# Attention, mixing and a Strassen feed-forward on one core: the mixing split in two, eight pairs of q left unscaled, and a new order table

## The chip, the cores and the metric

The kernel runs on one core of one Trainium2 chip. The metric is the device time of one execution in microseconds (us). The engines are named as the profile names them: PE is TensorE (PEld its weight loads), DVE is VectorE, ACT is ScalarE, POOL is GpSimd, SP is SyncE.

## The reference

Attention with a soft cap over 4 batches of 12 heads, 448 positions, 64 channels a head, then a block in which the positions are mixed through rank 32 and each position goes through a feed-forward layer of 768 to 3072 to 768 channels. All in float32.

```python
scale = 1.0 / np.sqrt(q.shape[-1])
scores = scale * np.matmul(q, k.transpose(0, 1, 3, 2))
scores = cap * np.tanh(scores / cap)
attn = np.exp(scores - np.max(scores, axis=-1, keepdims=True))
attn = attn / (np.sum(attn, axis=-1, keepdims=True) + 1e-09)
x = np.matmul(attn, v)                         # then heads side by side: [4, 448, 768]
...
xt = x.transpose(0, 2, 1)
h = xt @ U @ V                                 # U [448, 32], V [32, 448]
u = x + h.transpose(0, 2, 1)
out = u + np.maximum(u @ w_ch1, 0.0) @ w_ch2
```

## The kernel before, in words

Heads are taken in pairs, 24 pairs p in all, two heads in the 128 partitions of one tile: `qk` is [2 heads x 64, q or k, 448]. Each call of `four(p)` makes the work of four pairs. For each pair, score products of 128 keys at a time (L548) go into two PSUM banks, `tanh` reads them (L555, on ACT), one `exp` covers two such tiles (L566), and A·V products (L597) follow. The last 64 keys of two pairs share a tile (the rests: scores in tiles of 64x64, their A·V at L621). The finished sums of a pair are copied into `u[b]`, still unnormalized (a helper does every copy: L312 on ACT, L314 on DVE). The factor 1/(cap * sqrt(64)) of the scores is the column `qsc`: q of all pairs but the first is multiplied by it on DVE (L524); for the first pair, tanh takes it as its `scale`, from memory (`raw`).

`normalize(p)` works on two pairs. The row sums of exp are added up over tiles on DVE (L603, into `es`) and over partitions on PE (the sums, L646, tiles of 128x32, into the PSUM tile `misc`); they are copied to `sr`, spread by a transfer, inverted (L662), written to memory and read back broadcast as `rb`; then `u` is multiplied by `rb` (L675). Three transfers lie in that chain, on the queue of POOL.

`mixin(b, pp)` mixes one such two pairs, twelve times in all: 16 transposes (L696, tiles of 64x112), copies of them into `xx`, 8 U products (L712, tiles of 112x32), a copy into `ys`, 2 V products (L723, 64x128), and two adds onto `u` on DVE (L730). `misc` has two banks, and sums (one bank), transposes (two), U products (one) and V products (two) take turns in them.

After that, `moe` computes the feed-forward with Strassen's seven products in place of eight, both layers (L865 up, L1011 down), in products of 128x128 by 448 columns; operands are sums of blocks of `u` and of the weights, made on DVE, ACT and POOL, and stored and loaded through memory.

No order is written out by hand as a whole. Every piece of work is a `task` with a guessed duration, what it reads and writes, and a priority. `simulate()` plays the tasks through with the guessed durations and gives each a place in one program order. `NUDGE` changes some priorities, `SIDES` sets the engine of copies that ACT and DVE can both do, and `MOVES`, pairs (i, j), takes task i out of the order and puts it ahead of task j. The engines then run their instructions in that order and wait for one another by semaphores. A task's `mode` is the tile shape that the planner counts it under, and a name such as `("sums", p)` in a read list makes a task come behind the one that writes it.

Of the kernel before, what the change touches and what calls it, by code (L numbers as in the profile page):

```python
# [38 lines left out]
ALONE = 12  # L39


NUDGE = {89: 3, 194: 8, 248: -8, 361: -1, 440: 8, 653: 8, 717: -5, 782: -5, 823: 1}
MOVES = (
# [19 lines left out]
)  # L63
SIDES = {
    79: "DVE", 196: "DVE", 257: "DVE", 281: "ACT", 286: "ACT", 490: "ACT", 549: "ACT", 585: "ACT", 587: "ACT",
    625: "DVE", 666: "DVE", 670: "DVE", 774: "DVE",
}
NEXT = 8
LATER = 0
RESTS = 24  # L70
FILL, FIRST = 11, 3


# [245 lines left out]
class Build(Plan):  # L319
# [155 lines left out]
    def attention(self):  # L475

        u = self.u_bufs = [
            self.buf("u%d" % b, [128, NP, S], F32, self.ua if b < 2 else self.up) for b in range(B)]  # L480
        thirds = [lambda t, i=i: t[:, i:i + 2] for i in (0, 2, 4)]
        self.gw = Pool("gw", {"gq": 3}, after=(self.wx,), within=(self.wx, "x"), parts=(F32, [128, NP, S], {"gq": thirds}))
        self.es, self.rest = {}, {}
        for p in range(0, B * NP, 4):
            self.four(p)
            for q in (p, p + 2):
                self.normalize(q + 1)
                if q > 2:
                    self.mixin((q - 4) // NP, (q - 4) % NP // 2)
        for q in (B * NP - 4, B * NP - 2):  # L490
            self.mixin(q // NP, q % NP // 2)

    def psum(self, tag, n=1):
        pool = self.px if tag in ("sc2", "o2") else self.ps
# [2 lines left out]
    def four(self, p):  # L497
# [6 lines left out]
        for i in range(4):  # L504
            b, q = divmod(p + i, NP)
            if i % 2 == 0:
                vn = self.buf("vn", [128, 7, 2, D], F32, self.ap)
                vns.append(vn)
            qk = self.buf("qk", [128, 2, S], F32, *pools)
            qks.append(qk)  # L510

            if p + i == 0:
                cut = S + 128
                for a, z in ((0, cut), (cut, 2 * S)):
                    self.task({"SP": 350}, lambda a=a, z=z, b=b, q=q, qk=qk: nc.sync.dma_start(
                        out=qk.t.rearrange("p a s -> p (a s)")[:, a:z], in_=self.qk[b, q].rearrange("p a s -> p (a s)")[:, a:z]),
                        w=[(qk, 0 if a == 0 else "k")], lat=3400, prio=-2000 if a == 0 else prios[i])
                    if a == 0:
                        self.scales()
            else:  # L520
                self.task({"SP": 350}, lambda b=b, q=q, qk=qk: nc.sync.dma_start(out=qk.t, in_=self.qk[b, q]), w=[(qk, 0)],
                    lat=3400 if p == 0 else 4200, prio=prios[i])
            if p or i:
                self.task({"DVE": 360}, lambda qk=qk: nc.vector.tensor_scalar(  # L524
                    out=qk.t[:, 0], in0=qk.t[:, 0], scalar1=self.qsc, scalar2=None, op0=ALU.mult), r=[("scale", 0)], w=[(qk, 0)],
                    prio=prios[i])
            if i % 2:
                self.task({"SP": 350}, lambda b=b, q=q, vn=vn: nc.sync.dma_start(out=vn.t, in_=self.v[b, q // 2]),
                    w=[(vn, 0)], lat=4000, prio=prios[i], begin=6000 if p == 0 else 0)
# [3 lines left out]
        for g in range(7):  # L533
# [3 lines left out]
            for j in range(2):  # L537
# [11 lines left out]
                                ps.t[out, a, :S], qks[c].t[hd, 1, 128 * t:min(S, 128 * t + 128)], qks[c].t[hd, 0],  # L549
                                start=True, stop=True)  # L550

                raw = p == 0 and i == 0 or cs == (0, 1) and p == 0

                def tanh(j=j, ps=ps, th=th, raw=raw, t=t):
                    nc.scalar.activation(  # L555
                        out=th.t[:, j], in_=ps.t[:, :, :S], func=AF.Tanh, scale=(self.half if t == 3 else self.qsc) if raw else 1.0)

                r = [(qks[c], 0) for c in cs] + ([(qks[0], "k")] if p == 0 and t and 0 in cs else [])
                if j == 0:
# [120 lines left out]
    def mixin(self, b, pp):  # L680
# [15 lines left out]
                        nc.tensor.transpose(  # L696
                            tps[a].t[:TM, at:at + 64], u.t[hd, 2 * pp + i, TM * t:TM * t + TM], self.ident[hd, hd])

        self.task({"PE": 480}, transposes, r=[*ks, ("ident", 0)], w=[(tp, 0) for tp in tps], prio=prio, mode="sc")
        for a, tp in enumerate(tps):  # L700
            self.task({"ACT": 520, "DVE": 640}, lambda e, a=a, tp=tp: self.copy(
                e, xx.t.rearrange("p t i n -> p (t i) n")[:, :, 64 * a:64 * a + 64],
                tp.t[:TM].rearrange("p (m n) -> p m n", n=64)), r=[(tp, 0)], w=[(xx, a)], prio=prio)
        yp = self.psum("misc")

        def products():
# [5 lines left out]
                        nc.tensor.matmul(  # L712
                            yp.t[rows, :128], self.ust.t[:, t, :R], xx.t[:, t, i], start=h == 0, stop=h == 1)

        self.task({"PE": 450}, products, r=[(xx, 0), (xx, 1), (self.ust, 0), ("sums", p + 4)], w=[(yp, 0)], prio=prio - (20 if p < 19 else 0), mode="s")
        ys = self.buf("ys", [128, 128], F32, self.an)
        self.task({"ACT": 240, "DVE": 250}, lambda e: self.copy(e, ys.t, yp.t[:, :128]), r=[(yp, 0)], w=[(ys, 0)], prio=prio)
        hs = [self.psum("misc") for _ in range(2)]
# [375 lines left out]
```

## Time and profile before

| | us |
|---|---|
| median of 3 runs | 809.11 |
| lowest and highest | 808.36, 809.12 |
| the profiled execution | 810.04 |
| its span (first to last instruction) | 808.3 |
| busy in the span: PE, DVE, ACT, POOL | 798.9, 679.7, 472.0, 111.9 |

The busy times are for the whole span and hide that the attention part (to about 208 us) has other limits than the feed-forward behind it: ACT is busy 58% of the span, but nearly all of its first 60 us. A busy PE is one with work in its pipeline; PEld, the weight loads, overlaps it.

### The profile page before, as it was taken

What the parts mean: (1) busy time and instruction counts of PE and PEld (TensorE: products, weight loads), DVE (VectorE), ACT (ScalarE), POOL (GpSimd) and SP (SyncE); (2) the same over time, 40 slices, a digit from 0 to 9 for tenths busy, and PEclk for the clock granted to TensorE, in tenths of its full rate; (3) what the DMA queues carried; (4) which work ended last, traced back from release to release, by engine and by line L of the source; (5) the groups of instructions that cost most, each with busy time, mean ns of one, the idle gap of its engine ahead of it and who ended that gap; (6) DMA issues with size and microseconds to landing.
All of it is one profiled execution on the core that took longest, in us unless ns stands there. A gap on an engine that the chain in (4) does not pass through costs nothing.

```text
span 808.3 us, 11887 instructions
## 1 busy us (share of the span) xinstructions
PE 798.9 (99%) x4344; PEld 638.5 (79%) x4344; DVE 679.7 (84%) x1084; ACT 472.0 (58%) x669; POOL 111.9 (14%) x182
## 2 busy tenths in 40 slices
PE   9999999999999999999999999999999999999998
PEld 4333333437899999999999999999999999999997
DVE  3869999999999879998778683899999988897663
ACT  7999999976656455655555563435444543433330
POOL 0111111111111111111111121011100011000100
PEclk9999999999999999999999999999999999999999
DMA  7365575315877888547777864966973688524142
GB/s 236 118 215 157 168 232 138 117 47 151 290 270 258 296 298 286 198 139 237 276 259 236 280 209 135 388 219 166 367 244 104 163 260 256 150 61 115 38 134 92
DMA packets 54525, 161.76 MB, mean 200 GB/s; under 512 B 7458, under 2 KB 21314, under 8 KB 54466
## 3 DMA queue, kind: packets, MB, share of 16 engines
q1 hardware_dynamic: 34736, 106.82, 40.6%
q0 software_dynamic: 12816, 35.30, 15.3%
q10 hardware_dynamic: 6914, 18.88, 5.9%
q8 instruction: 34, 0.56, 0.3%
q14 instruction: 25, 0.20, 0.1%
HBM read 106.81 MB, written 46.49 MB: 190 GB/s over the span
## 4 chain that ended last, share of the span: by engine, by line
PE 83%; DVE 8%; ACT 4%; DMA 3%; issue 2%; POOL 0%; ACTq 0%; DVEq 0%; POOLq 0%
PE mm L1011 38%; PE mm L865 36%; PE sc L548 4%; DVE es L603 3%; PE o L597 3%; ACT th L555 2%; DMA r<-sr 2%; DMA qk<-in_qk 1%; ACT th L566 1%; DVE u L730 1%; DMA mid<-cx 1%; PE misc L468 1%; DVE ws L763 1%; PE misc L723 1%; DVE u L675 1%
## 5 line engine op out<-in xcount | busy, mean ns | idle before, releaser
L865 PE MATMUL mm<-x,ws 128*128 128x448 f32 x1404 | 288.8, 365 | 0.4 <-ACT cx L312 0.3
L865 PEld LDWEIGHTS mm<-x,ws 128*128 128x128 f32 x1404 | 262.7, 188 | 24.8 <-ACT cx L312 1.9
L1011 PE MATMUL mm<-g,wl 128*128 128x448 f32 x570 | 148.9, 364 | 0.0
L1011 PEld LDWEIGHTS mm<-g,wl 128*128 128x128 f32 x570 | 107.0, 188 | 8.7
L1031 DVE TENSOR_TENSOR u<-u,mm 128x448 f32<-128x448 f32 x111 | 67.5, 616 | 41.0 <-PE mm L1011 38.4
L1011 PE MATMUL mm<-g,bw 128*128 128x448 f32 x420 | 101.4, 366 | 0.0
L891 POOL DMA_DIRECT2D mid<-cx x96 | 54.0, 562 | 256.8 <-ACT cx L312 246.8
L1011 PEld LDWEIGHTS mm<-g,bw 128*128 128x128 f32 x420 | 78.9, 188 | 6.3
L1011 PE MATMUL mm<-gk,bw 128*128 128x448 f32 x336 | 83.0, 367 | 0.0
L548 PE MATMUL sc<-qk 64*128 64x448 f32 (+1 forms) x384 | 77.6, 569 | 0.3 <-ACT th L555 0.3
L312 ACT ACTIVATE cx<-mm 128x448 f32<-128x448 f32 x96 | 48.8, 543 | 47.6 <-PE mm L865 32.3
L566 ACT ACTIVATE th<-th,capt 128x1792 f32<-128x1792 f32 x42 | 75.5, 1798 | 0.9
L555 ACT ACTIVATE th<-sc 128x896 f32<-128x896 f32 x80 | 69.8, 919 | 4.9 <-PE sc L548 4.6
L1011 PEld LDWEIGHTS mm<-gk,bw 128*128 128x128 f32 x336 | 63.1, 188 | 5.5
L312 ACT ACTIVATE cx<-cx 128x448 f32<-128x448 f32 x72 | 41.6, 577 | 43.6 <-DVE cx L878 40.5
L1036 POOL DMA_DIRECT2D u<-st x33 | 28.5, 875 | 247.0 <-ACT st L312 229.3
L878 DVE TENSOR_TENSOR cx<-cx,mm 128x448 f32<-128x448 f32 x72 | 44.4, 617 | 20.9 <-PE mm L865 18.1
L548 PEld LDWEIGHTS sc<-qk 64*128 64x128 f32 (+1 forms) x384 | 27.7, 175 | 41.5 <-issue 21.0
L597 PE MATMUL o<-th,vn 128*64 128x448 f32 x280 | 57.9, 548 | 0.9 <-ACT th L566 0.9
L312 ACT ACTIVATE st<-mm 128x448 f32<-128x448 f32 x33 | 17.9, 544 | 68.9 <-PE mm L1011 31.0
L603 DVE TENSOR_TENSOR es<-es,th 128x896 f32<-128x896 f32 (+1 forms) x48 | 51.8, 1079 | 4.7 <-ACT th L566 4.0
L1011 PE MATMUL mm<-gk,wl 128*128 128x448 f32 x186 | 55.8, 365 | 0.0
(110 smaller groups left out, 1039.1 us busy)
## 6 DMA issues: line engine op xcount, KB each, us to landing
wr<-in_w SPq DMA_DIRECT2D x48, 768.0 KB, 6.1
mid<-cx POOLq DMA_DIRECT2D x96, 224.0 KB, 4.0
gq<-mid SPq DMA_DIRECT2D x44, 448.0 KB, 7.0
qk<-in_qk SPq DMA_DIRECT2D x23, 448.0 KB, 4.1
kept<-wa ACTq DMA_DIRECT2D x24, 384.0 KB, 6.3
quad<-wa ACTq DMA_DIRECT2D x24, 384.0 KB, 6.2
wb<-quad SPq DMA_DIRECT2D x24, 384.0 KB, 8.4
wa<-kept SPq DMA_DIRECT2D x24, 384.0 KB, 4.4
```

The source lines that it names most:

```text
L312: e.activation(out=out, in_=in_, func=func)
L548: nc.tensor.matmul(ps.t[out, a, :S], qks[c].t[hd, 1, 128 * t:min(S, 128 * t + 128)], qks[c].t[hd, 0], start=True, stop=True)
L555: nc.scalar.activation(out=th.t[:, j], in_=ps.t[:, :, :S], func=AF.Tanh, scale=(self.half if t == 3 else self.qsc) if raw else 1.0)
L566: nc.scalar.activation(out=th.t, in_=th.t, func=AF.Exp, scale=self.capt)
L597: nc.tensor.matmul(o.t[64 * a:64 * a + 64, :S], vn.t[:, 3 * i + t, a], th.t[:, j, a], start=t == 0, stop=False)
L603: e.tensor_tensor(out=out(), in0=in0(), in1=in1(), op=ALU.add)
L865: nc.tensor.matmul(ps.t[:, :S], ws[p].t[:, wi, sl], xs[p].t[:, xi, d], start=fresh and n == 0, stop=n == 8, skip_group_check=not fresh)
L878: self.task({"DVE": 630}, lambda: nc.vector.tensor_tensor(out=to(x), in0=to(x), in1=bank[onto].t[:, :S], op=ALU.add), r=[key(x), (bank[ont ...
L891: nc.gpsimd.dma_start(out=self.mid[at][:, c % 2], in_=to(x))
L1011: nc.tensor.matmul(ps.t[:, :S], w[p, m].t[:, wi, k, sl], g[p, n, m][gi].t[:, k], start=fresh and i == 0, stop=i == len(at) - 1, skip_group ...
L1031: self.task({"DVE": 622}, lambda: nc.vector.tensor_tensor(out=out(), in0=out(), in1=ps.t[:, :S], op=ALU.add), r=[(ps, 0)], w=[key], prio=-200)
L1036: self.task({"POOL": 1000}, lambda: nc.gpsimd.dma_start(out=out(), in_=st.t, accum_op=ALU.add), r=[(st, 0)], w=[key], lat=5000, size=1360, ...
```

## The change

First, `mixin` stops once, between the copies of the transposes and the U products, and `attention` runs the first half of one mix ahead of the sums of a later two pairs and its second half behind them: the mix is now that of six pairs back (it was four). The U products wait for the sums of that later pair by name, where they waited for an earlier one, and have no priority of their own any more. Three mixes are left for the end of attention, where there were two. Second, q of the pairs from `PLAIN` = 16 on is not multiplied on DVE; their 28 tanh take `qsc` as `scale`. Third, `NUDGE` is empty and `MOVES` and `SIDES` hold other numbers.

```diff
-NUDGE = {89: 3, 194: 8, 248: -8, 361: -1, 440: 8, 653: 8, 717: -5, 782: -5, 823: 1}
+NUDGE = {}
 MOVES = (
-    (1993, 1994), (1974, 1993), (1997, 2001), (1992, 1997), (1928, 1989), (1985, 1972), (1969, 1983), (1970, 1969),
...
+    (2046, 2070), (2003, 2025), (2023, 2024), (2018, 1999), (2021, 2018), (2002, 2021), (1964, 2015), (1929, 1964),
...
+PLAIN = 16
...
             for q in (p, p + 2):
+                mixed = self.mixin((q - 6) // NP, (q - 6) % NP // 2) if q >= 6 else iter(())
+                next(mixed, None)
                 self.normalize(q + 1)
-                if q > 2:
-                    self.mixin((q - 4) // NP, (q - 4) % NP // 2)
-        for q in (B * NP - 4, B * NP - 2):
-            self.mixin(q // NP, q % NP // 2)
+                next(mixed, None)
+        for q in (B * NP - 6, B * NP - 4, B * NP - 2):
+            for _ in self.mixin(q // NP, q % NP // 2):
+                pass
...
-            if p or i:
+            if (p or i) and p < PLAIN:
                 self.task({"DVE": 360}, lambda qk=qk: nc.vector.tensor_scalar(
...
-                raw = p == 0 and i == 0 or cs == (0, 1) and p == 0
+                raw = p == 0 and i == 0 or cs == (0, 1) and p == 0 or p >= PLAIN
...
-                        out=th.t[:, j], in_=ps.t[:, :, :S], func=AF.Tanh, scale=(self.half if t == 3 else self.qsc) if raw else 1.0)
+                        out=th.t[:, j], in_=ps.t[:, :, :S], func=AF.Tanh, scale=(self.half if t == 3 and p == 0 else self.qsc) if raw else 1.0)
...
+        yield
         yp = self.psum("misc")
...
-        self.task({"PE": 450}, products, r=[(xx, 0), (xx, 1), (self.ust, 0), ("sums", p + 4)], w=[(yp, 0)], prio=prio - (20 if p < 19 else 0), mode="s")
+        self.task({"PE": 450}, products, r=[(xx, 0), (xx, 1), (self.ust, 0), *([("sums", p + 6)] if p + 6 < B * NP else [])], w=[(yp, 0)], prio=prio - 0, mode="s")
```

In the rows below `misc`, `sc` and `o` are PSUM tiles (a number marks which one of several), and a row such as "128x448 x2" is two instructions of 128 by 448. Lines after L524 stand three to five further down in the changed kernel: L548 is L551, L597 is L600, L646 is L649, L696 is L699, L712 is L716 and L723 is L727.

On PE, in the middle of attention, around one round of sums, transposes, U and V products. Before:

```order
L646 MATMUL misc<-es,ones 32x448 x4
L548 MATMUL sc<-qk 128x448 x2
L548 MATMUL sc_1296<-qk 128x448 x2
L696 MATMUL misc<-ident,u_1016 112x64 x16
L597 MATMUL o<-th,vn 64x448 x6
L712 MATMUL misc<-xx,ust 32x128 x8
L548 MATMUL sc<-qk 128x448 x2
L548 MATMUL sc_1358<-qk 128x448 x2
L723 MATMUL misc<-vst,ys 128x448 x2
L597 MATMUL o_1381<-th,vn 64x448 x6
```

And of the change:

```order
L649 MATMUL misc<-es,ones 32x448 x4
L716 MATMUL misc<-xx,ust 32x128 x8
L551 MATMUL sc<-qk 128x448 x2
L551 MATMUL sc_1286<-qk 128x448 x2
L727 MATMUL misc<-vst,ys 128x448 x2
L600 MATMUL o<-th,vn 64x448 x6
L699 MATMUL misc<-ident,u_996 112x64 x16
L551 MATMUL sc<-qk 128x448 x2
L551 MATMUL sc_1346<-qk 128x448 x2
L600 MATMUL o_1360<-th,vn 64x448 x6
```

The U products have moved up to the sums. The transposes of the next mix stand where V products of this one are one A·V task back.

On PE, at the end of attention, where the first products of the feed-forward (L865, now L869) come in. Before:

```order
L696 MATMUL misc<-ident,u_1016 112x64 x16
L597 MATMUL o<-th,vn 64x448 x6
L597 MATMUL o_1623<-th,vn 64x448 x6
L712 MATMUL misc<-xx,ust 32x128 x8
L621 MATMUL o<-th,vn 64x448 x2
L621 MATMUL o_1623<-th,vn 64x448 x2
L723 MATMUL misc<-vst,ys 128x448 x2
L865 MATMUL mm<-x,ws 128x448 x9
L646 MATMUL misc<-es,ones 32x448 x4
L865 MATMUL mm<-x,ws 128x448 x9
```

And of the change:

```order
L727 MATMUL misc<-vst,ys 128x448 x2
L600 MATMUL o<-th,vn 64x448 x6
L699 MATMUL misc<-ident,u_996 112x64 x16
L600 MATMUL o_1609<-th,vn 64x448 x6
L624 MATMUL o<-th,vn 64x448 x2
L624 MATMUL o_1609<-th,vn 64x448 x2
L869 MATMUL mm<-x,ws 128x448 x9
L649 MATMUL misc<-es,ones 32x448 x4
L716 MATMUL misc<-xx,ust 32x128 x8
L869 MATMUL mm<-x,ws 128x448 x9
L727 MATMUL misc<-vst,ys 128x448 x2
```

V products and transposes stand ahead of the last A·V task, where the U products stood behind it.

On ACT, between three of the last dozen exps (L566, now L569; tanh is L555, now L558; copies are L312, now L313). Before:

```order
L566 ACTIVATE th<-th,capt 128x1792
L555 ACTIVATE th<-sc 128x896
L555 ACTIVATE th<-sc_1266 128x896
L312 ACTIVATE u_1016<-o 128x448
L312 ACTIVATE u_1016<-o_1248 128x448
L312 ACTIVATE sr<-misc 128x448
L566 ACTIVATE th<-th,capt 128x1792
L312 ACTIVATE xx<-misc 112x8x64
L555 ACTIVATE th<-sc 128x896
L555 ACTIVATE th<-sc_1296 128x896
L312 ACTIVATE bx<-xc 128x448
```

And of the change:

```order
L569 ACTIVATE th<-th,capt 128x1792
L558 ACTIVATE th<-sc,qsc 128x896
L558 ACTIVATE th<-sc_1240,qsc 128x896
L313 ACTIVATE u_996<-o_1226 128x448
L313 ACTIVATE sr<-misc 128x448
L313 ACTIVATE ys<-misc 128x128
L569 ACTIVATE th<-th,capt 128x1792
L558 ACTIVATE th<-sc,qsc 128x896
L558 ACTIVATE th<-sc_1286,qsc 128x896
L313 ACTIVATE x<-u_271 128x448
```

Every tanh there takes `qsc`; one copy into `u`, the copy of transposes and the one into `bx` are gone from this piece, and one of U products and one of `x` have come.

## Rows read from the trace of the kernel before

**Rows 1.** The first line of the profile's page.

```profile
span 808.3 us, 11887 instructions
```

**Rows 2.** Stretches: length, busy us of PE, PEld, DVE, ACT, POOL; granted clock; DMA.

```profile
8.08:61.45 53.37, 52.71 (x319) 19.17 (x318) 36.83 (x54) 52.62 (x50) 6.56 (x11) 1.00 0.56 177
61.45:131.50 70.05, 69.06 (x526) 26.55 (x524) 67.11 (x102) 64.77 (x69) 11.60 (x20) 1.00 0.57 175
131.50:175.06 43.56, 42.54 (x308) 16.38 (x304) 43.33 (x70) 43.29 (x49) 6.76 (x12) 1.00 0.37 106
175.06:208.37 33.31, 31.52 (x242) 21.40 (x242) 32.41 (x58) 20.90 (x44) 5.99 (x11) 1.00 0.57 167
208.37:804.60 596.23, 596.20 (x2934) 550.62 (x2934) 497.95 (x792) 286.95 (x457) 80.32 (x125) 1.00 0.66 214
```

**Rows 3.** Waits of PE, 17 to 209 us: total, times, longest.

```profile
PE o L597 <- ACT th L566: 0.9, 1, 0.9
PE misc L723 <- ACT ys L312: 0.9, 2, 0.5
PE misc L723 <- DVE ys L314: 0.8, 3, 0.4
PE misc L646 <- DVE u L730: 0.5, 1, 0.5
PE misc L696 <- DVE u L675: 0.4, 1, 0.4
PE sc L548 <- ACT th L555: 0.3, 1, 0.3
PE misc L712 <- DVE xx L314: 0.2, 1, 0.2
```

**Rows 4.** Timeline of PE, 149 to 172 us: start, us, engine and line.

```profile
149.97 1.77 PE L548 MATMUL sc<-qk 64*128 64x448 f32 x8
151.68 0.98 PE L621 MATMUL o<-th,vn 64*64 64x448 f32 x8
...
155.97 2.48 PE L597 MATMUL o<-th,vn 128*64 128x448 f32 x12
158.38 0.64 PE L712 MATMUL misc<-xx,ust 112*32 112x128 f32 x16
158.95 1.77 PE L548 MATMUL sc<-qk 64*128 64x448 f32 x8
160.56 0.92 PE L723 MATMUL misc<-vst,ys 64*128 64x448 f32 x4
161.31 1.67 PE L548 MATMUL sc<-qk 64*128 64x448 f32 x8
...
168.82 1.77 PE L548 MATMUL sc<-qk 64*128 64x448 f32 x8
170.43 0.62 PE L696 MATMUL misc<-ident,u 64*112 64x64 f32 x16
170.98 1.35 PE L597 MATMUL o<-th,vn 128*64 128x448 f32 x6
```

**Rows 5.** Groups by line and form, whole span: busy us, mean ns.

```profile
L555 ACT ACTIVATE th<-sc 128x896 f32<-128x896 f32 x80 | 69.8, 919 | 4.9 <-PE sc L548 4.6
...
L524 DVE TENSOR_SCALAR qk<-qk,qsc 128x448 f32<-128x448 f32 x23 | 10.0, 440 | 8.3 <-DMA qk<-in_qk 8.2
...
L555 ACT ACTIVATE th<-sc,qsc 128x896 f32<-128x896 f32 x3 | 3.0, 1002 | 3.2 <-PE sc L548 3.2
```

**Rows 6.** The same view for ACT, 131.5 to 175.06 us.

```profile
L312 ACT ACTIVATE u<-o 128x448 f32<-128x448 f32 x5 | 2.7, 570 | 0.0
...
L312 ACT ACTIVATE bx<-xc 128x448 fp32r<-128x448 f32 x1 | 0.6, 637 | 0.0
```

**Rows 7.** Timeline, 102 to 108 us.

```profile
103.05 1.67 PE L548 MATMUL sc<-qk 64*128 64x448 f32 x8
...
106.36 1.15 DVE L730 TENSOR_TENSOR u<-u,misc 128x448 f32<-128x448 f32 x2
```

More of the change, by code (lines that the diff above doesn't have):

```diff
@@ L39 @@
 ALONE = 12
-NUDGE = {89: 3, 194: 8, 248: -8, 361: -1, 440: 8, 653: 8, 717: -5, 782: -5, 823: 1}
+NUDGE = {}
 MOVES = (
[19 rows of a table removed]
[19 rows of a table added]
 )
 SIDES = {
-    79: "DVE", 196: "DVE", 257: "DVE", 281: "ACT", 286: "ACT", 490: "ACT", 549: "ACT", 585: "ACT", 587: "ACT",
-    625: "DVE", 666: "DVE", 670: "DVE", 774: "DVE",
+    79: "DVE", 80: "ACT", 171: "DVE", 263: "ACT", 279: "ACT", 360: "DVE", 370: "ACT", 562: "ACT", 577: "ACT",
+    579: "ACT", 587: "ACT", 593: "ACT", 595: "ACT", 625: "ACT", 656: "DVE", 662: "DVE", 670: "ACT",
 }
@@ L697, in transposes @@
                             tps[a].t[:TM, at:at + 64], u.t[hd, 2 * pp + i, TM * t:TM * t + TM], self.ident[hd, hd])
-        self.task({"PE": 480}, transposes, r=[*ks, ("ident", 0)], w=[(tp, 0) for tp in tps], prio=prio, mode="sc")
+        self.task({"PE": 480}, transposes, r=[*ks, ("ident", 0)], w=[*((tp, 0) for tp in tps), ("turned", p)], prio=prio, mode="sc")
         for a, tp in enumerate(tps):
```

36 rows, old and new, of the table MOVES are left out of this document.

## The prediction, made before the changed kernel was run

> **What bounds the kernel now.** The page's first line gives the span, 808.3 us [rows 1]; the profiled execution took 810.04 us in all, 1.74 us more, and the median of the runs shown is 809.11 us, 0.93 us under it. My sum is made against 810.04, and 0.93 is taken off at the end. I call a difference under 0.2% (1.6 us) no change, which is about what a measurement of this kernel can tell.
>
> I cut the attention and what follows into stretches and asked for the busy time of each engine in them [rows 2]. The reader is to see that the limit changes. From 8 to 61 us ScalarE is busy 52.62 of 53.37 us: tanh and exp set the pace. From 61 to 131 us TensorE is busy 69.06 of 70.05 us and ScalarE has 5.28 us free. From 131 to 175 us, where the last exp ends, ScalarE is busy 43.29 of 43.56 us, VectorE 43.33, and TensorE 42.54: all three are full. From 175 to 208 us the tail of the mixing lies between the first of the large products, and TensorE idles 1.8 us. From 208 us to the last product it idles 0.03 of 596 us. The granted clock is 1.00 (the 2.4 GHz level) in every stretch, so no stage of it can become faster by a better clock. All that the change can win or lose therefore lies ahead of 208 us: whatever brings the first uninterrupted large product forward by one microsecond brings the end forward by one.
>
> The waits of TensorE between 17 and 209 us say where it stood still [rows 3]: seven kinds, ten waits, 4.0 us. And TensorE's own timeline in a regular part [rows 4] says what it pays without a wait. There a pair of score products starts at 149.97 and the next task at 151.68: 1.71 us. From 158.95 to 160.56 and from 168.82 to 170.43 it is 1.61 us. The first pair has another tile shape ahead of it (A·V, 128\*64) and another one behind (64\*64). The second has a U product of 112\*32 in front, but behind it the V products, which have its own 64\*128. In the third the transposes, 64\*112, follow as cheaply as the V products. So I read 0.10 us on each side where the shape changes, 0.20 us for a change, and none between 64\*128 and 64\*112.
>
> **Step 1, the U products behind row sums.** The U products (112\*32) stood alone between scores, A·V or rests. Nine of the twelve now come directly behind row sums (128\*32). No matmul is added or removed. Counting tile shapes in the order of both kernels, with 112 and 128 rows or columns as one, the changes outside the warm-up fall from 114 to 106. The upper bound of the gain is 8 x 0.20 = 1.6 us [rows 4]; if only one side of each goes, it is 8 x 0.10 = 0.8; and 0 if 112 rows behind 128 rows is a change like any other, for no row of before shows such a neighbour. I take the middle of the first two, **-1.2 us**.
>
> The Trainium skill says, on the page TensorEngine Tiling (Array Packing), section Key Properties: "Mode switching requires drain: Changing tiling mode (not just tile) drains the TensorE". The trace agrees, with the 0.10 us on a side above. That page counts modes in rows of 128, 64 and 32, by which 112\*32 behind 128\*32 is no switch; no row here shows that pair.
>
> **Step 2, TensorE's waits.** Taken from [rows 3] one by one. The sums waited 0.5 us for an add of the mixing, since sums, transposes, U and V products share two banks; the sums now come behind scores and rests that follow the transposes, long after the adds, so -0.5. The U products waited 0.2 us for the copy of the transposes; the transposes now lie over 10 us ahead of them, -0.2. The transposes waited 0.4 us for a normalizing multiply, which sums, reciprocal and three transfers precede; they now belong to a mix one pair of pairs older, -0.4. The longest, 0.9 us, is the last A·V task's wait for the last exp; V products and transposes now stand ahead of it, which take 0.75 us (160.56 to 161.31) and 0.55 us (170.43 to 170.98) [rows 4], so -0.9. The V products' waits for a copy of the U result stay where U and V are neighbours (two places in the tail, 0.9 us behind ScalarE); of those behind VectorE, 0.8 us, I take half, -0.4, because two score tasks now stand between as a rule. Against that, there are three runs of four score tasks instead of one. A fourth score task needs a bank that a tanh still reads: 0.3 us for the one of before, so up to 0.6 more, and 0.5 with the transposes that lie in one of them. Net **-1.9 us**; at worst none of it goes, at best all 4.0.
>
> **Step 3, q unscaled.** Eight multiplies on VectorE go, each 440 ns [rows 5], 3.5 us busy. VectorE does not set the end by itself, so I count this as the cover of step 2: without it the adds and copies above would be later. In exchange 28 tanh take their factor from a column in memory. The three early ones that do so took 1002 ns against 919 [rows 5], so +83 ns each. Four of them fall before 131 us, where ScalarE has 5.28 us free: nothing. Twenty-four belong to the last dozen exps, in the stretch where it has 0.27 us free or just ahead of it: 24 x 0.083 = 2.0 us. There ScalarE also loses work: the other operations between these exps fall from 20 to 14, mostly copies that take 0.57 to 0.64 us [rows 6]; six at 0.6 are -3.6 us. So its own load there falls by 1.6 us.
>
> The Trainium skill speaks against this part: the page ScalarE: Activation LUTs, section What ACT_TABLE_LOAD costs, gives about 93 ns for each one-column pointer operand of an activation. By that, an estimate, the 28 would cost 2.6 us, and by the row 2.3; the trace agrees nearly.
>
> **Step 4, what the full stretch gives back.** Between 131 and 175 us TensorE may not run ahead of ScalarE. Of steps 1 and 2 some 1.6 us would be saved there (two or three mixes' shape changes, 0.4; the 0.9 us wait, and 0.3 of others). ScalarE's own 1.6 us less would just let that through. But VectorE, as full as they, takes over copies of 0.6 us and gives up multiplies of 0.44 there, so I let a third of it be lost: **+0.5 us**. Should the copies not help ScalarE at the point where it holds the others up, the 1.6 us are lost and the 2.0 us of the tanh come on top: that is the bound, +3.6.
>
> **Step 5, the rest.** The normalizing chain, its queue on GpSimd, SyncE's loads and the Strassen products keep their order but for small exchanges, and TensorE waits for none of them after 208 us [rows 2]: 0. This holds as long as the large products of the first minutes find their operands; if the new table makes one late, it counts one for one.
>
> **Sum.** -1.2 - 1.9 + 0.5 = -2.6 us: 807.4 for the profiled execution, less 0.93: **806.5 us**; I round to 806.6.
>
> **The rivals.**
>
> *A, slower: the transposes wait for the adds.* In before, other work stood between the V products and the next transposes. Now one A·V task (2.41 us, 155.97 to 158.38 [rows 4]) or two score tasks do. The transposes write both shared banks, and the two adds must have read them. At one mix of before the V products ended at 103.05 and the second add at 107.51 [rows 7], 4.5 us later, behind other VectorE work. There transposes would wait 2.1 us with all that is queued behind them on TensorE, A·V and scores, and so ScalarE too. Three such make 6.3 us: 807.4 + 6.3 - 0.93 = 812.8. It decides from a total of about 4 us on. For it: VectorE is 96% to 99% busy from 61 to 175 us. Against it: most adds of before end sooner, and VectorE has 3.5 us less to do.
>
> *B, the same: ScalarE holds attention.* If it is the bound from 131 us and also carries over what TensorE gains before, only the tail wins: the 0.9 us wait and a few changes, -1.1: 808.0. For it: three engines are full at once. Against it: the 5.28 us free before.
>
> *C, the change does not do what it says:* 112 rows behind 128 cost a change. Step 1 is 0: 807.7.
>
> *D, more: every wait goes,* and no step is given back: -1.6 - 4.0 + 0.6 (the runs of four scores) = -5.0, which is 804.1. For it: VectorE is relieved ahead of every wait named.
>
> **How the numbers follow.** The forecast 0.47, A 0.12, B 0.20, C 0.06, D 0.15. The range must leave out no more than 2 in 10: A lies beyond it, with the outermost of D. Its lower end is D and 0.3 us (803.8); its upper end is the forecast with the worst of step 4 (806.6 + 3.6 = 810.2). Faster by over 0.2% is below 807.5: D, nine tenths of the forecast, little of the others: 0.60. Within 0.2% lie B, C and the rest of the forecast with a part of A: 0.27. Slower is most of A and some of step 4's bound: 0.13.
>
> **What would show it.** Step 1: the U products start 0.9 us behind the sums, and take under 0.5 us to the next start. Step 2: the rows of [rows 3] for sums, transposes and the last A·V are gone; scores waiting for tanh are up to 1 us. Step 3: tanh with the column at 1000 ns, 31 of them. Step 4: the last exp ends about 2 us earlier than 175.06, and ScalarE is still full from 131 us on. Step 5: from about 205 us TensorE runs without a gap, at 1.00. Wrong would be: a row in which transposes wait for the adds (A); a last exp that ends no earlier (B); a gap in TensorE after 208 us.

## The result

| | before | after |
|---|---|---|
| median, 4 runs each on one chip, us | 809.12 | 814.0 |
| lowest and highest, us | 808.36, 810.03 | 813.03, 814.55 |
| span of the profiled execution, us | 808.3 | 812.6 |

The ratio is 1.0056, 95% interval 1.0043 to 1.0069: the changed kernel is slower by 4.5 us (3.5 to 5.6). The forecast was 806.6, the range ended at 810.2.

The changed kernel's stretches, cut at the same times as [rows 2] (length, busy us of PE, PEld, DVE, ACT and POOL, granted clock, DMA):

```profile
8.08:61.45 53.37, 52.74 (x306) 19.45 (x306) 35.91 (x51) 52.54 (x52) 6.16 (x10) 1.00 0.55 180
61.45:131.50 70.05, 68.87 (x529) 27.04 (x526) 64.39 (x98) 68.44 (x71) 11.73 (x20) 1.00 0.57 188
131.50:175.06 43.56, 43.35 (x328) 16.66 (x324) 43.06 (x69) 42.41 (x46) 7.47 (x12) 1.00 0.31 87
175.06:208.37 33.31, 30.94 (x241) 21.47 (x238) 32.91 (x57) 21.72 (x44) 5.58 (x10) 1.00 0.56 169
208.37:808.90 600.53, 597.84 (x2933) 549.76 (x2931) 504.78 (x800) 283.69 (x449) 79.61 (x125) 1.00 0.65 212
```

The last row is the surprise. TensorE, which idled 0.03 us behind 208 us, now idles 2.7. In the four rows ahead of it, it idles 0.6, 1.2, 0.2 and 2.4 us, 4.4 in all; in [rows 2] it was 0.7, 1.0, 1.0 and 1.8, 4.5. The idle time ahead of 208 us moved out of the full stretch into the tail and hardly shrank.

TensorE's waits of the changed kernel from 17 to 209 us (total, times, longest), to be read against [rows 3], which leaves out one row of the kernel before (the first one here):

```profile
PE mm L865 <- ACT cx L312: 0.3, 1, 0.3
```

```profile
PE sc L551 <- ACT th L558: 1.0, 3, 0.5
PE misc L727 <- ACT ys L313: 0.9, 2, 0.5
PE mm L869 <- ACT cx L313: 0.7, 1, 0.7
PE mm L869 <- ACT u L313: 0.7, 1, 0.7
PE misc L727 <- DVE ys L315: 0.4, 1, 0.4
```

And from 209 us to the end, where the kernel before has none:

```profile
PE mm L869 <- ACT cx L313: 1.9, 3, 0.7
PE mm L869 <- DVE cx L882: 0.7, 1, 0.7
```

These are four places, on TensorE's timeline:

```profile
406.80 1.48 PE L869 MATMUL mm<-x,ws 128*128 128x448 f32 x6 [0.58 <-ACT cx L313]
453.48 1.28 PE L869 MATMUL mm<-x,ws 128*128 128x448 f32 x5 [0.68 <-ACT cx L313]
...
496.38 2.09 PE L869 MATMUL mm<-x,ws 128*128 128x448 f32 x9 [0.68 <-ACT cx L313]
499.19 2.09 PE L869 MATMUL mm<-x,ws 128*128 128x448 f32 x9 [0.71 <-DVE cx L882]
```

Ahead of 209 us the waits of the sums, U products and transposes and the one for the last exp are gone. In their place the first large product waits 0.7 us for the copy of the last A·V result, and a later one 0.7 (the kernel before: 0.3) for a copy `cx` out of its bank. All named waits up to 209 us fall from 4.3 to 3.7 us.

How much of the lead reaches the end of the mixing is seen on TensorE's timeline. First the kernel before, then the changed one; left out are the rounds between:

```profile
177.35 0.98 PE L621 MATMUL o<-th,vn 64*64 64x448 f32 x8
178.26 1.02 PE L723 MATMUL misc<-vst,ys 64*128 64x448 f32 x4
179.21 2.08 PE L865 MATMUL mm<-x,ws 128*128 128x448 f32 x9
181.22 0.96 PE L646 MATMUL misc<-es,ones 128*32 128x448 f32 x8
...
210.33 1.97 PE L865 MATMUL mm<-bx,ws 128*128 128x448 f32 x9
```

```profile
175.45 0.98 PE L624 MATMUL o<-th,vn 64*64 64x448 f32 x8
177.10 2.09 PE L869 MATMUL mm<-x,ws 128*128 128x448 f32 x9 [0.66 <-ACT u L313]
179.12 0.96 PE L649 MATMUL misc<-es,ones 128*32 128x448 f32 x8
179.90 0.62 PE L716 MATMUL misc<-xx,ust 112*32 112x128 f32 x16
...
209.75 1.99 PE L869 MATMUL mm<-bx,ws 128*128 128x448 f32 x9
```

The first large product starts 2.1 us earlier. But before, the U and V products of one more mix lay ahead of it (0.58 and 0.95 us); now they lie behind it. At the same product `bx` behind the last V products, the lead is 0.6 us.

The rows that answer to [rows 5] (busy us, mean ns):

```profile
L558 ACT ACTIVATE th<-sc 128x896 f32<-128x896 f32 x52 | 44.9, 912 | 0.9 <-PE sc L551 0.7
...
L558 ACT ACTIVATE th<-sc,qsc 128x896 f32<-128x896 f32 x31 | 29.8, 1017 | 4.0 <-PE sc L551 4.0
```

A tanh with the column costs 105 ns more, not 83.

### The profile page after: what moved, and what is told of

The parts are those of the page before. It is cut to its first block, busy times and chain, and to the rows that moved or that the text cites. A ratio compares the mean times of both kernels' runs of the same rounds, so it can differ in the third digit from the quotient of the medians.

```text
span 812.6 us, 11845 instructions
## 1 busy us (share of the span) xinstructions
PE 800.6 (99%) x4344; PEld 638.4 (79%) x4344; DVE 683.1 (84%) x1083; ACT 472.0 (58%) x662; POOL 111.2 (14%) x182
## 4 chain that ended last, share of the span: by engine, by line
PE 87%; DVE 6%; ACT 3%; issue 2%; DMA 1%; POOL 0%; DVEq 0%; POOLq 0%; ACTq 0%
PE mm L1015 38%; PE mm L869 36%; PE sc L551 5%; PE o L600 4%; DVE es L606 3%; ACT th L558 1%; PE misc L727 1%; DMA mid<-cx 1%; PE misc L649 1%; PE o L624 1%; ACT th L569 1%; PE misc L469 1%; PE misc L699 1%; ACT cx L313 0%; DMA qk<-in_qk 0%
## 5 line engine op out<-in xcount | busy, mean ns | idle before, releaser
L869 PE MATMUL mm<-x,ws 128*128 128x448 f32 x1404 | 290.9, 366 | 4.1 <-ACT cx L313 2.6
L869 PEld LDWEIGHTS mm<-x,ws 128*128 128x128 f32 x1404 | 262.3, 188 | 31.5 <-ACT cx L313 5.1
L1015 PEld LDWEIGHTS mm<-g,wl 128*128 128x128 f32 x582 | 109.3, 188 | 8.9
L1015 PE MATMUL mm<-g,bw 128*128 128x448 f32 x414 | 96.8, 366 | 0.0
L313 ACT ACTIVATE cx<-mm 128x448 f32<-128x448 f32 x96 | 47.5, 544 | 59.0 <-PE mm L869 46.7
L551 PE MATMUL sc<-qk 64*128 64x448 f32 (+1 forms) x384 | 78.1, 573 | 1.3 <-ACT th L558 1.3
L569 ACT ACTIVATE th<-th,capt 128x1792 f32<-128x1792 f32 x42 | 75.4, 1796 | 1.0
L313 ACT ACTIVATE cx<-cx 128x448 f32<-128x448 f32 x72 | 41.6, 578 | 36.1 <-DVE cx L882 35.3
L313 ACT ACTIVATE st<-mm 128x448 f32<-128x448 f32 x33 | 18.0, 544 | 73.3 <-PE mm L1015 43.1
L551 PEld LDWEIGHTS sc<-qk 64*128 64x128 f32 (+1 forms) x384 | 27.6, 176 | 40.6 <-issue 21.2
L600 PE MATMUL o<-th,vn 128*64 128x448 f32 x280 | 57.9, 548 | 0.0
L767 DVE TENSOR_TENSOR ws<-ta,ws 128x384 fp32r<-128x384 f32 x96 | 52.9, 553 | 3.4 <-ACT ws L313 2.4
L373 ACT ACTIVATE wa<-wr 128x768 f32<-128x768 f32 (+2 forms) x50 | 44.3, 888 | 18.3 <-DMA quad<-wa 5.4
```

Of the source, the lines that this page charges most:

```text
L313: e.activation(out=out, in_=in_, func=func)
L373: nc.scalar.activation(out=a_t(), in_=raw_t()[:, 1::2].bitcast(F32), func=AF.Prelu, scale=2.0 ** -112, alpha=-(2.0 ** 32))
L551: nc.tensor.matmul(ps.t[out, a, :S], qks[c].t[hd, 1, 128 * t:min(S, 128 * t + 128)], qks[c].t[hd, 0], start=True, stop=True)
L569: nc.scalar.activation(out=th.t, in_=th.t, func=AF.Exp, scale=self.capt)
L600: nc.tensor.matmul(o.t[64 * a:64 * a + 64, :S], vn.t[:, 3 * i + t, a], th.t[:, j, a], start=t == 0, stop=False)
L767: e.tensor_tensor(out=lo, in0=src(), in1=hi.bitcast(F32), op=ALU.subtract)
```

## The experiments

**Exchanging what lies behind the mixing.** The order, engines and buffers of everything behind the last add of the mixing were taken from the other kernel, as tables of task numbers, engines and buffer places; up to there nothing changes. The same edit makes both kernels, on the changed kernel and on the one before:

```diff
             first()
+            order = order[:CUT] + [self.tasks[i] for i in TAIL]
+            for i, e in ENGINES:
+                self.tasks[i].eng = e
+            for tag, i, p, slot in HOMES:
+                x = self.order[tag][i]
+                x.pool, x.slot = POOLS[p], slot
             for t in order:
```

New attention with the late order of before:

> The changed kernel up to the last add of the mixing, and from there on the order, engines and buffers of the kernel before, for everything that is left. Theory (the 4.9 us lost behind 208 us come from the order that the new table and the planner give the products, copies and loads there): TensorE runs without waits from 215 us on as in the kernel before, and the time is 814.0 - 4.9 = 809.1, or down to 808.5. Rival (the new attention leaves loads, weights or buffers late, and any order behind it has to wait): waits of 3 to 4 us remain behind 208 us, 812 to 814.

Attention of before with the late order of the change:

> The reverse: the kernel before up to the last add of the mixing, and from there on the order, engines and buffers of the changed kernel. Theory: the waits of the changed kernel behind 350 us come along, 4.2 us, and the slightly longer product, 0.6: 809.1 + 4.9 = 814.0. Rival (they belong to the new attention): no waits behind 208 us, 809 to 810.

Measured, with 809.3 for the kernel before on that chip: 809.44, ratio 1.001 (1.000 to 1.0019), and 812.49, ratio 1.0046 (1.0033 to 1.0058). The stretches from 208 us show where (columns as above; first the new attention with the old late order, then the reverse):

```profile
208.37:500.00 291.63, 291.63 (x1440) 269.96 (x1439) 239.35 (x474) 160.93 (x296) 51.11 (x91) 1.00 0.70 243
```

```profile
208.37:500.00 291.63, 289.89 (x1421) 265.99 (x1420) 244.24 (x478) 156.96 (x287) 49.83 (x91) 1.00 0.69 242
```

So the waits follow the late order, whichever attention is ahead of it. By the ratios the late order costs 3.7 us in either pairing (2.7 to 4.7 behind the attention of before), and the new attention by itself 0.8 (0 to 1.5; the medians differ by 0.1). The two make the 4.5 of the change. The traces agree without the attention: from the end of the last V products to the last product it is 596.5 us in the kernel before and 596.0 in the first exchange, 601.0 in the changed kernel and 600.2 in the reverse. The theory held; the reverse came out 1.5 under its 814.0, in part because the wait near 453 us was 0.3 us shorter in its trace and the one near 406 absent.

**A product right behind its own bank's copy, six times.** In the kernel before, product 3 ahead of product 6 in six chunks:

```diff
 MOVES = (
...
+    (1394, 1392), (1486, 1484), (1578, 1576), (1675, 1673), (1772, 1770), (1864, 1862),
 )
```

> The kernel before with product 3 moved ahead of product 6 in six chunks of the first layer (13, 15, 17, 19, 21, 23), so that in each of them products 6 and 7, which add into one PSUM bank with a copy of it between, follow each other directly. Theory (such a neighbour costs the copy and its two handings-over, 0.95 us, as at 496 and 498 us in the changed kernel): 6 x 0.95 = 5.7 us, 814.8. Rival (the wait is made good where TensorE next would have waited): below 812, since TensorE waits nowhere else there it should not be.

814.08 against 809.04: 5.0 us, 0.84 each (by the ratio, 1.0065, 1.0048 to 1.0081, 0.65 to 1.1 each). TensorE's waits from 209 us, and one of the places:

```profile
PE mm L866 <- ACT cx L313: 4.1, 6, 0.7
```

```profile
362.68 1.38 PE L866 MATMUL mm<-x,ws 128*128 128x448 f32 x6
...
364.14 0.54 ACT L313 ACTIVATE cx<-mm 128x448 f32<-128x448 f32 x1 [1.91 <-PE mm L866]
...
364.74 1.50 PE L866 MATMUL mm<-x,ws 128*128 128x448 f32 x6 [0.68 <-ACT cx L313]
```

Products 6 and 7 add into one bank, and the copy `cx` has to read it between them. With a product between them that is hidden; without one TensorE stands for 0.68 us. Nothing later makes that good, since TensorE waits nowhere else there. The loss is more than the wait. The matmuls of a product start 203 ns apart but take 366 ns each, and a wait counts from the end of the last one, so 0.16 us come on top; the next start is 0.31 us off as well, not 0.20. That is the theory's 0.95 us a place, inside the interval. The changed kernel has two such neighbours at the end of the first layer (products 6, 7 and 4 of the last chunk in a row, the waits at 496 and 499 us). The order of before had products of the second layer (L1011) ahead of the last one:

```profile
495.05 1.40 PE L1011 MATMUL mm<-gk,wl 128*128 128x448 f32 x6
...
497.51 1.98 PE L865 MATMUL mm<-x,ws 128*128 128x448 f32 x9
```

**Moving three products.** In the changed kernel, product 6 ahead of product 3 in the chunks with waits:

```diff
 MOVES = (
...
+    (1522, 1524), (1711, 1713), (1854, 1856),
 )
```

> The changed kernel with product 6 of three of the 24 chunks of the first layer (numbers 16, 20 and 23) placed ahead of product 3 instead of behind it; nothing else moves. Theory (the loss behind 208 us is a few products that come too close to the PSUM copy or the buffer that they need): the waits of 0.73, 0.84 and 0.84 us at 406, 453 and 496 us go, with 0.1 each in the products behind them; the wait of 0.88 at 498 stays. 814.0 - 2.7 = 811.3. Rival (the weights or the transfers of that part are late because of what the new attention left behind, and the products only show it): the waits turn up one or two products later, and the time stays within 1 us of 814.0.

813.3, where 811.3 was expected; ratio 1.0054 (1.0039 to 1.0069), no different from the change. The waits at 406 and 496 us are gone. The one at 499 was left alone, the one at 453 stays, with one of 0.25 us at 463. And in the profiled execution the gain was spent in the tail. TensorE there, and ScalarE's queue:

```profile
202.36 0.66 PE L700 MATMUL misc<-ident,u 64*112 64x64 f32 x16
204.93 1.28 PE L870 MATMUL mm<-x,ws 128*128 128x448 f32 x5 [1.91 <-ACT cx L314]
```

```profile
201.26 0.91 ACT L374 ACTIVATE wa<-wr 128x768 f32<-128x768 f32 x1 [3.74 <-DMA wr<-in_w]
202.07 0.51 ACT L314 ACTIVATE ws<-ta 128x384 fp32r<-128x384 f32 x1
...
202.95 0.56 ACT L314 ACTIVATE cx<-cx 128x448 f32<-128x448 f32 x1
203.42 1.03 ACT L314 ACTIVATE x<-u 128x448 fp32r<-128x448 f32 x2
```

The copy that the product needs stands in ScalarE's queue behind a weight conversion that waits for a load. In the profile of the changed kernel the same conversion waits 1.7 us and no product waits there; here it is 3.7, and the product waits 1.9. The order is the same in both up to there: a load that lands later by some 2 us in one execution is hidden or not. That execution took 814.19 us, 0.9 above the median; whether the others lost their gain there is not shown.

At 453 us the reason is another one, on ScalarE in the changed kernel:

```profile
452.88 0.98 ACT L313 ACTIVATE cx<-mm 128x448 f32<-128x448 f32 x2 [1.31 <-DMA mid<-cx]
453.74 0.53 ACT L313 ACTIVATE ws<-wa 128x384 fp32r<-128x384 f32 x1
```

As I read this row, the copy has no `cx` buffer until an earlier result has been stored, and moving a product does not give it one. No run gave it one, so this is not shown.

**The last chunk spread out.** As above, with (1854, 1850), (1849, 1854), (1860, 1856) and (1855, 1860) for its last pair.

> As the run with three products moved, and in the last chunk products 6 and 7 are spread so that another product stands between each two that use the same PSUM bank (1, 6, 2, 7, 3, 4). Theory: the fourth wait, 0.88 us at 498 us, goes too: 814.0 - 3.7 = 810.3. Rival (late operands): weights of products 6 and 7 are asked for earlier and come no sooner, so a wait of about a product, 1 to 2 us, takes its place: 811.5 to 813.

814.5, ratio 1.007 (1.0058 to 1.0082). The two waits at 496 and 498 us became one of 1.3 us for an add near 497, with 0.3 behind it for a weight of the second layer, and 1.1 us for a copy near 451. The rival was right in its direction, too low in its 811.5 to 813, and its late weight shows only in the 0.3 us: the products gained no room by coming sooner.

**ScalarE's queue.** In the changed kernel, the copy at 406 us ahead of the conversion that it stood behind, and the conversion at 202 us behind the copy:

```diff
 MOVES = (
...
+    (1523, 1602), (806, 766),
 )
```

> The changed kernel with two ScalarE instructions put back in its queue: near 406 us a weight conversion (wa from wr) goes behind the copy that empties the PSUM bank of product 6 of chunk 16, where it stood ahead of it, and near 202 us another such conversion, which waits for a load, goes behind the copy out of product 4 of chunk 0. No product moves. Theory (products wait because the copy that frees their bank stands in ScalarE's queue behind an instruction that waits for something else): the wait of 0.73 us at 406 goes with 0.1 behind it, and 0.16 to 2.0 us at 202, which differed from run to run with that load: 812.3 to 813.0. Rival (the copies are late for another reason): 814.0 and the wait at 406 stays.

813.72, ratio 1.0059 (1.0047 to 1.0071). The wait at 406 us is gone, so there the copy's place in the queue was the cause. At 202 us the conversion now ran right ahead of the copies of the last transposes, and U products waited 0.6 us for those. No gain in sum.

**The tail.** The first exchange with the second of these moves, and U products ahead of the first large product: `(806, 766), (570, 681),`.

> The run with the new attention and the late order of before, with the conversion near 202 us moved behind the copy as in the run beside it, and the U products behind the last sums moved ahead of the first large product, which waits 0.7 us for the copy of the last A·V result. Theory: 0.57 us of that wait is filled by the U products, and 0.2 to 0.6 us go at 202: 809.4 - 0.9 = 808.5, which would be under the kernel before. Rival (what is gained there is waited for in the next products, whose operands come from the same mixing): 809.4.

810.08, ratio 1.0012 (1.0003 to 1.0021): no gain. The wait of 0.7 us for the A·V copy went; U products wait 0.6 for the copies of transposes, and transposes 0.3 for that of the sums. The rival was right in that. No kernel of this study is faster than the one before.

**U products away from the sums.** In the changed kernel six mixes' U products moved ahead of the rests: `(272, 248), (369, 345), (384, 356), (462, 438), (477, 449), (555, 531),`.

> The changed kernel with the U products of six mixes moved from directly behind the row sums to directly ahead of the rests that stand before those sums: 12 tile-shape changes more, the same matmuls. By the prediction's price of 0.15 to 0.20 us a change the attention part gets 1.8 to 2.4 us longer: 816. By the price read in the changed kernel's trace (the sums of four matmuls take 0.11 us less to the next start when U products follow), 1.3 us: 815.3. Rival (ScalarE sets the pace and a shape change costs nothing that is not waited away): 814.0.

814.55, ratio 1.0066 (1.0053 to 1.0078), 0.8 us above the change by the ratios, within the intervals: the time decides between none of the three. My 12 was wrong: the traces count 120 shape changes up to the product `bx` against 110, ten more. The rows decide. One round, first in the changed kernel and then here:

```profile
121.96 0.96 PE L649 MATMUL misc<-es,ones 128*32 128x448 f32 x8
122.74 0.62 PE L716 MATMUL misc<-xx,ust 112*32 112x128 f32 x16
123.29 1.94 PE L551 MATMUL sc<-qk 64*64 64x448 f32 x12
```

```profile
121.60 0.98 PE L625 MATMUL o<-th,vn 64*64 64x448 f32 x8
122.51 0.96 PE L650 MATMUL misc<-es,ones 128*32 128x448 f32 x8
123.40 1.94 PE L552 MATMUL sc<-qk 64*64 64x448 f32 x12
```

Sums take 0.78 us to the next start with U products behind them, and 0.89 with scores: 0.11 us a change, which 112 rows behind 128 do not pay.

**Unscaled q alone,** in the kernel before, in its own order and tables. The multiply of a pair from 16 on is not issued:

```diff
-                self.task({"DVE": 360}, lambda qk=qk: nc.vector.tensor_scalar(
+                self.task({"DVE": 360}, lambda qk=qk, p=p: p < PLAIN and nc.vector.tensor_scalar(
...
-                        out=th.t[:, j], in_=ps.t[:, :, :S], func=AF.Tanh, scale=(self.half if t == 3 else self.qsc) if raw else 1.0)
+                        out=th.t[:, j], in_=ps.t[:, :, :S], func=AF.Tanh, scale=(self.half if t == 3 and p == 0 else self.qsc) if raw or p >= PLAIN else 1.0)
```

> The kernel before in its own order and tables, with only the second part of the change: q of the last eight pairs is not multiplied on VectorE, and their 28 tanh take the column as scale. Theory (the tanh's 83 ns fall into a stretch where ScalarE has 0.27 us free): the last exp ends 1.5 to 2.3 us later, and as the tail of the mixing has other work the end moves by 1 to 2 us: 810.1 to 811.1. Rival (VectorE's 3.5 us less are worth as much as ScalarE's 2.3 us more): 809.1 within 0.5.

810.59 against 809.24, ratio 1.0017 (1.0007 to 1.0027): it costs 1.4 us (0.6 to 2.2). The theory held on the sum, not on its way there: the last exp starts at 174.04 instead of 173.28, 0.8 us later and not 1.5 to 2.3.

**The multiplies put back,** on the first exchange, from a table of places in the order; the 28 tanh lose their column:

```diff
             for t in order:
+                if t.i in AHEAD:
+                    qk = self.order["qk"][AHEAD[t.i]]
+                    self.nc.vector.tensor_scalar(out=qk.t[:, 0], in0=qk.t[:, 0], scalar1=self.qsc, scalar2=None, op0=ALU.mult)
                 for b in t.bufs:
```

> As the first of these three, and the second part of the change undone: the eight multiplies of q stand on VectorE again, three VectorE operations ahead of where the first scores of each pair are issued, and the 28 tanh have no column. What is left of the change is the split mixing with its table up to 208 us. Theory (the column costs 0.5 us up to the last exp, as the run of that part alone showed, and about 1.3 us in the median): 0.5 to 1.3 us below the first of these three, 808.0 to 808.5. Rival (VectorE is the narrower of the two in the new order): the same as the first or up to 1 us longer.

> The run with the multiplies put back on VectorE, which stood so late in its queue that scores waited for them (4.8 us), once more with the multiplies twelve VectorE operations ahead of each pair's first scores instead of three. Theory (the column costs ScalarE about 0.5 to 1.3 us, and the multiplies nothing when they stand early): 808.0 to 809. Rival (VectorE is so full in the new order that 3.5 us more of it moves everything, wherever they stand): over 811.

816.11, ratio 1.0087 (1.0071 to 1.0103), with the multiplies three VectorE operations ahead of the scores, and 816.59, ratio 1.0102 (1.0082 to 1.0123), with twelve: by the ratios 6 to 7.5 us above the kernel without them, where 0.5 to 1.3 below was expected. In the first, scores stand for 4.8 us in which the profile names no releaser; the multiply is what they lacked by the order. In the second the leading waits of TensorE up to 221 us are others:

```profile
PE misc L999 <- DVE sr L587: 2.3, 2, 2.1
PE misc L971 <- DVE u L1006: 1.4, 2, 0.8
PE mm L1141 <- ACT cx L585: 1.2, 2, 0.9
```

The second of them is rival A's: transposes (L971) wait for adds (L1006). But neither place was a fair one. In the second run VectorE itself stood 3.2 us in front of two multiplies whose q had not landed:

```profile
L572 DVE TENSOR_SCALAR qk<-qk,qsc 128x448 f32<-128x448 f32 x8 | 3.6, 456 | 3.2 <-DMA qk<-in_qk 3.2
```

In the first, the longest wait was followed by a fall of TensorE's granted clock, from 1.00 ahead of it to 0.50 (the 1.2 GHz level). Scores that take 1.94 us elsewhere took 3.57:

```profile
169.28 3.57 PE L823 MATMUL sc<-qk 64*128 64x448 f32 x12 [3.13 <-issue]
```

```profile
169.28:172.80 3.52, 3.52 (x16) 1.23 (x20) 2.43 (x5) 0.92 (x1) 0.00 (x0) 0.50 0.02 5
```

The three executions of each run whose mean granted clock is 0.999 or 1.000 took 814.54 to 815.40 us, the others 816.82 to 820.27. So these two places cost eight multiplies of 0.44 us more than their own time, part of it through the clock; what a better place would cost is not shown. Whether an order made for them carries them is left to the next three.

**Without tables.** `NUDGE`, `MOVES` and `SIDES` empty, so that the planner's own order runs: the kernel before, the split alone (`PLAIN = 24`), and the whole change.

> The kernel before with its three tables emptied, so that the planner's own order runs. It is the base of the two runs beside it; both theories expect it above 809, by some us.

> The changed kernel's split mixing alone: tables empty, all q multiplied on VectorE. Theory (the split by itself saves shape changes worth 0.9 us and moves waits about, and what it does to the rest is a matter of the order that the planner and the table make of it): within 2 us of the kernel before with empty tables. Rival (the split itself costs, and the table of the changed kernel only hides it): 3 us or more above it.

> The changed kernel with empty tables. Theory (unscaled q alone costs 1 us or so where VectorE has room, and pays where the split mixing leaves it none): between 2 us below and 1 us above the split alone. Rival (it costs ScalarE time in any order): 1 to 2 us above the split alone.

816.9, 821.75 and 822.1, with ratios to the kernel before of 1.0105 (1.0081 to 1.0128), 1.0159 (1.0144 to 1.0174) and 1.017 (1.0134 to 1.0207). The split costs 4.4 us under the planner's own order, outside my theory and by the rival's number. But most of it is not lost where the split is: from the end of the last V products to the last product it is 598.86 us in the kernel before without tables and 599.94 with the split, which by then has nine matmuls (1.83 us) fewer left to do. So 2.9 us lie behind the attention, where the exchanges point at the late order, here the planner's own; no run without tables exchanged it. What the other 1.5 us are was not settled: the granted clock differs there as well, 0.96 from 176 to 217 us in the profile of the first, which took 820.13 us, and 1.00 in that of the second. Unscaled q on top of the split costs nothing that these runs can tell, so there the multiplies cost no more than the column. And TensorE's waits behind 225 us in the whole change without tables are the kinds that the table left in:

```profile
PE mm L846 <- ACT cx L290: 1.0, 2, 0.7
PE mm L846 <- DVE cx L859: 0.7, 1, 0.7
```

## Why the prediction was wrong

**Step 5 failed, and most of the result is its.** It put everything behind 208 us at nothing, from a row of the kernel before, and noted that a late operand would count one for one. The late order was not the same: the new table ordered it too, and the prediction's own sign for this, a gap in TensorE after 208 us, came. That costs 3.7 us, shown by both exchanges. Of its mechanisms, the direct neighbours (0.84 us each, put into the kernel before) and the copy behind a conversion (its wait went when it was moved) were shown; that for want of a `cx` buffer was only read from the trace. No run that took single waits out of the changed kernel was faster for it clear of the intervals; other waits came in their place. The wait rows name 2.6 us. In the trace, the starts of two products stand 0.94 to 1.08 us apart at the four waits and 0.31 at the next pair, in place of 0.20: 3.7 us. The rest is spread over the products (last section). Without tables, too, 2.9 us of the split's 4.4 are lost behind the attention.

**Step 1 was right in kind and a third too large.** Sums followed by U products save 0.11 us. Eight changes fewer are 0.9, not 1.2; the U products themselves take 0.55 us to the next start, not under 0.5. Rival C fell.

**Step 2 named the waits rightly and missed the new ones.** Every wait that it took off is gone, and the scores' waits are the 1.0 that it allowed. But the two of 0.7 us, of large products for ScalarE, were not in it: of one kind no row showed a wait before, and the other's 0.3 us is the row that [rows 3] leaves out, so that its seven kinds and 4.0 us were eight and 4.3. The named waits fell by 0.6 us in place of 1.9, and TensorE's idle time up to 208 us by 0.1. The error was to take a wait that ends as time won: TensorE came to the large products earlier and stood there for ScalarE instead.

**Step 3 had the price too low:** 105 ns a tanh instead of 83, 2.9 us for 28. By itself the part costs 1.4 us. ScalarE's lighter load from 131 us on was paid for earlier: from 61 to 131 us it is busy 68.44 us in place of 64.77. That the part was the cover of the other steps is not shown: without it, in this order, the kernel loses 6 to 7.5 us, but in places where scores waited for the multiplies or VectorE for a load, and in part through the clock; under the planner's own order the multiplies cost no more than the column.

**Step 4's** reading of the last exp was right: it starts at 171.20 instead of 173.28, 2.1 us earlier, as the prediction's list of signs asked. Its use of it was wrong. U and V products worth 1.5 us had gone behind the first large product, and 0.6 us of lead were left. Rival B, only the tail wins, comes nearest for attention, though the new attention by itself (0 to 1.5 us slower) did not win even that. The profiled execution of before was 0.9 us above its median, so its 0.6 us of lead is not at odds with that. How the 0.8 us of the new attention divide among shape changes, tanh and waits was not settled.

**Rival A fell.** No row in the changed kernel has transposes waiting for the adds; they do wait, 1.4 us, where the multiplies were put back early.

## What to carry to other kernels

A table that sets the order is part of the change everywhere that it orders, not only where the idea lies: walk through the new order to its end, and at each accumulating bank ask what stands between the two writers. An engine whose idle time is zero for 600 us is where an order can only lose. And a lead at one event (the last exp) is worth what the same work, counted from there to the end, still leaves of it.

## What the runs showed of the hardware

Executions that are alike up to there set in at different times. The first exp of a full tile starts at 8.39 us in the profile of the changed kernel and at 7.73 in that with U products moved, whose order first differs much later; and ScalarE waited 1.7 or 3.7 us for one and the same load near 200 us. A single row can carry that much.

Between 216 and 350 us, where no kernel waits, the matmuls of the large products start 203.8 ns apart in both kernels with the late order of the change and 203.2 ns apart in both with that of before (the mean over some 660 starts in each trace). That makes 0.4 us there. Why was not settled.
